# Backward attention loop: dS turned by the DMA alone, loads in groups, dK and dV stored once per head group

## The chip, the cores and the metric

The kernel runs on one core of a Trainium2 chip. The metric is device time in microseconds (us) of one execution, as a median of several runs. One more execution was taken by the hardware profiler; all durations, waits and busy shares come from that one, and its span is set beside the median of the runs below.

The engines of the core have their own instruction queues: TensorE (PE, with PEld for its weight loads), VectorE (DVE), ScalarE (ACT), GpSimd (POOL), and SyncE (SP), which only issues DMAs. A DMA that ScalarE issues stands in ScalarE's own queue between its other instructions.

## The reference

A transformer block (adaptive layer norm, multi-head attention, squared-ReLU MLP) is run forward, and all its gradients are computed. Sizes: 2048 tokens, model width 512, 32 heads of 16, hidden width 1792, bf16.

```python
def _A_ref(x, wqkv, wo):
    qkv = (x @ wqkv).reshape(B, S, 3, H, Dh).transpose(2, 0, 3, 1, 4)
    q, k, v = (qkv[0], qkv[1], qkv[2])
    scores = jnp.einsum('bhqd,bhkd->bhqk', q, k) * Dh ** (-0.5)
    p = softmax(scores, axis=-1)
    o = jnp.einsum('bhqk,bhkd->bhqd', p, v)
    return o.transpose(0, 2, 1, 3).reshape(B, S, D) @ wo
...
h = _layernorm(x) * (1 + ca) + sa
x = x + ga * _A_ref(h, A_wqkv, A_wo)
h = _layernorm(x) * (1 + cb) + sb
x = x + gb * _B_ref(h, B_w1, B_b1, B_w2, B_b2)
...
_out, _vjp = jax.vjp(_f, A_x, A_wqkv, A_wo, B_w1, B_b1, B_w2, B_b2, c, w_mod)
return (_out, *_vjp(grad_out))
```

The change concerns the gradient of the attention: with P the softmax and dP = dO V^T, dS = P * (dP - delta), and from it dQ = dS K, dK = dS^T Q and dV = P^T dO.

## The kernel before

The kernel has three parts in time: the forward pass with the MLP and its gradients (to about 1117 us), the backward attention loop (about 1117 to 2387 us), and a last stage that multiplies by the transposed wqkv, finishes the layer norm's gradient and forms the gradients of wqkv and w_mod (to the end).

**Tiling of the loop.** Heads are taken in eight groups of four (`hg`). For a group the keys are cut into four chunks of 512 (`kc`), the queries into four chunks of 512 (`qc`), and these into four tiles of 128 (`qi`). A *unit* is one (hg, kc, qc, qi): 128 queries by 512 keys by four heads. Four units with the same qc are a *block*; there are 512 units and 128 blocks, 16 blocks to a head group. Each operand of a group lies in a tile of 128 partitions, 32 to a head: 16 rows of data and one more that carries the softmax's normalization or delta, so that the matmul of scores already holds the shift and the matmul of dP already holds the subtraction of delta.

**One unit.** TensorE makes four score products (`score`, L1594, into one of three PSUM banks), ScalarE takes the exponential of each (`expo`, L1600, the tile `E_u`), TensorE makes dP for two heads at a time (`dp_pair`, L1614, `psD_u`), and VectorE multiplies the two (L1616, the tile `dS_u`, 128 x 1024 for two heads). `k_quad` (L1654) and `v_quad` (L1663) accumulate dK and dV of the group over all 16 query tiles in one bank, `accVK`, which ScalarE copies out for each key chunk into `vkb` (L1666).

**Turning dS.** dQ needs dS with keys on the partitions. Two units of a block share a `dS_u` tile (four such tiles go round), and after the second one SP issues a DMA transpose of the tile into `dsT` (L1631, 128 x 4096 bf16 or 1.05 MB; three `dsT` tiles go round, one for each block). So blocks with an even number make two such transposes. In blocks with an odd number (`on_pe`) the first two units go that way, the third goes by a DMA transpose of its own of half the size (L1629), and the fourth is turned on TensorE: `pe_turn` (L1644) makes eight 128 x 128 transposes into a PSUM bank, twice, and ScalarE copies each result out into `dsT` (L1760). A block's dQ (`dq_quad`, L1681, `dqacc`) is made two blocks later, ScalarE scales it into `dqtmp` or `dQacc` (L1694, L1691), and GpSimd adds it (L1699).

**Order.** The order of instructions on all five engines in the loop is written out by hand: two strings of tokens, `order_t` for the block after an odd one and `order_n` for the other. A token is a step: `s` a score, `e` an exponential, `D` a `dp_pair` with its product on VectorE and, after every other unit, the transpose; `q` a `k_quad` or `v_quad`; `d` half of a dQ; `Q` its eviction. Only `order_t` has `t` and `T` (TensorE's turn and its eviction) and `f` (`keep_warm`, filler matmuls, L1637). Both strings hold eight `D` for each block, so 128 to a head group.

**Transfers of the loop.** The calls `at(j, load, ...)` put a DMA behind the j-th `D`, in ScalarE's queue (`load`, L1576). `plan_head` plans the loads of the next head group: `kvq_loads` (q of the group with tokens on the partitions as `qs`, then k, q with its normalization row, v) and the rows of dO and delta; 22 loads, one every four `D`, from the 14th of the group before. Two sets of tiles (`hsets`) alternate between the groups. `spread_qz` (GpSimd) spreads `qs` into `qz` at `D` number 40 after that start. The finished dK and dV of a key chunk are stored four `D` after their eviction, 128 KB each time (`dVKtP`), and dQ of a group goes out in four stores from the sixth `D` after its last block (`dQc`). `head_loads` makes the loads of group 0 from SP's queue, before the loop, with the same `kvq_loads`. In the last group SP also loads finished gradients for the last stage.

All DMAs of SP and ScalarE draw their completion semaphores in turn from eight, so that a DMA first waits for the one that had its semaphore before it.

Of the kernel before, what the change touches and what calls it, by code (L numbers as in the profile page):

```python
# [34 lines left out]
def kernel(  # L35
# [9 lines left out]
    QC = n // 512  # L45
# [43 lines left out]
    q_st = dram.tile([HG, P, TT, 64], BF, name="q_st")  # L89
# [17 lines left out]
    dVKtP = dram.tile([HG, P, n], BF, name="dVKtP")  # L107
# [23 lines left out]
    def row_loads(dst, srcT, hg, cols, aux=None):  # L131
        for h in range(4):
            i = hg * 4 + h
            yield dst[32 * h:32 * h + DH, :], srcT[i * DH:(i + 1) * DH, cols]
        if aux is not None:
            yield dst.rearrange("(h c) n -> c h n", h=4)[DH], aux[hg * 4:(hg + 1) * 4, cols]
# [10 lines left out]
    with ExitStack() as ph:  # L147
# [969 lines left out]
        loads = {}  # L1117
# [85 lines left out]

        def kvq_loads(hg):
            hs = hsets[hg % 2]
            for i in range(4):
                yield hs["qs"][:, 4 * i:4 * i + 4, :], q_st[hg][:, 4 * i:4 * i + 4, :]
            yield from row_loads(hs["k"], qkT_st[1], hg, slice(0, n))
            yield from row_loads(hs["q"], qkT_st[0], hg, slice(0, n), m_st)
            yield from row_loads(hs["v"], vT_st, hg, slice(0, n))  # L1210
# [282 lines left out]
        with ExitStack() as ph2:  # L1493
            pools["mm"] = ph2.enter_context(tc.tile_pool(name="psM2", bufs=4, space=bass.MemoryType.PSUM))
            with tc.manual_schedule(engines={PE.engine, ACT.engine, DVE.engine, SP.engine, POOL.engine}):
# [28 lines left out]
                def head_loads():  # L1524
                    done = slice(0, 512 * (QC - 1))
                    for i, (to, fro) in enumerate(list(kvq_loads(0)) + list(row_loads(hsets[0]["do"][:, done], dOT_st, 0, done, d_st))):
                        later(i, sp, to, fro)
                    later(12, copy_const, qz[0].rearrange("p t h d -> p (t h d)"), 0.0)
                    later(16, spread_qz, 0)
# [18 lines left out]
    with ExitStack() as ph:  # L1548
# [7 lines left out]
        hst, bst, sst, dqt, cur = {}, {}, {}, {}, {}  # L1556
# [12 lines left out]
        def at(j, f, *args):  # L1569
            todo.setdefault(j, []).append((f, args))  # L1570
# [7 lines left out]
        def plan_head(hg):  # L1578
            j0 = (hg - 1) * 128 + 14
            loads = list(kvq_loads(hg)) + list(row_loads(hsets[hg % 2]["do"], dOT_st, hg, slice(0, n), d_st))  # L1580
            for i, (to, fro) in enumerate(loads):
                at(j0 + 4 * i, load, to, fro)
            at(j0 + 40, spread_qz, hg)

        banks = {"A": "ps0", "B": "ps1", "C": "px"}
# [16 lines left out]
        def dp_pair(u, pair):  # L1602
            hg, kc, qc, qi = units[u]
            st = hst[hg]
            qt = qc * 4 + qi
            if pair == 0:
                if qi % 2 == 0:
                    cur["dS"] = ework.tile([P, 2, 4, 512], BF, name="dS_u", tag="dS_u", bufs=4)
                bst[u][1] = cur["dS"][:, qi % 2]
            E_u, dS_u = bst[u]  # L1610
            psD = psd.tile([P, 2, 512], F32, name="psD_u", tag="pd")
            for hi in range(2):
                r = 32 * (2 * pair + hi)
                PE.matmul(psD[:, hi, :], st["do"][r:r + 32, qt * P:(qt + 1) * P], st["v"][r:r + 32, kc * 512:kc * 512 + 512],  # L1614
                          start=True, stop=True, tile_position=(r, 0))
            DVE.tensor_tensor(dS_u[:, 2 * pair:2 * pair + 2, :], psD[:], E_u[:, 2 * pair:2 * pair + 2, :], ALU.mult)  # L1616
            if qi == 3 and on_pe(u // 4):
                held["dS"] = dS_u

        def on_pe(b):  # L1620
            return b % 2 == 1

        def transpose_unit(u):
            hg, kc, qc, qi = units[u]
            if qi == 0:
                dqt[u // 4] = tpool.tile([P, 4, 16, P], BF, name="dsT", tag="dsT")
            if on_pe(u // 4) and qi >= 2:
                if qi == 2:
                    SP.dma_start(out=dqt[u // 4][:, qi], in_=bst[u][1].rearrange("p h k -> p (h k)"), transpose=True)  # L1629
            elif qi % 2 == 1:  # L1630
                SP.dma_start(out=dqt[u // 4][:, qi - 1:qi + 1].rearrange("p u b q -> p (u b) q"),  # L1631
                             in_=cur["dS"].rearrange("p u h k -> p (u h k)"), transpose=True)
# [24 lines left out]
        def v_quad(u):  # L1657
            hg, kc, qc, qi = units[u]
            qt = qc * 4 + qi
            E_u, dS_u = bst.pop(u)  # L1660
            acc = cur["vk"]
            for hq in range(4):
                PE.matmul(acc[32 * hq:32 * hq + DH, :], dOs_tok[:, qt, (hg * 4 + hq) * DH:(hg * 4 + hq + 1) * DH], E_u[:, hq, :],  # L1663
                          start=False, stop=(qt == TT - 1), tile_position=(0, 32 * hq), skip_group_check=True)
            if qt == TT - 1:
                ACT.activation(hst[hg]["vk"][:, kc * 512:(kc + 1) * 512], acc[:], AF.Identity)  # L1666
                if hg >= HG - 2:
                    xs["vk", hg] = hst[hg]["vk"]
                else:
                    part = slice(kc * 512, (kc + 1) * 512)  # L1670
                    at(cur["j"] + 4, load, dVKtP[hg][:, part], hst[hg]["vk"][:, part])

        def dq_quad(b, kt):
            hg, kc, qc, _ = units[4 * b]
# [40 lines left out]
        for hg in range(1, HG):  # L1715
            plan_head(hg)
# [3 lines left out]
        with tc.manual_schedule(engines={PE.engine, ACT.engine, DVE.engine, SP.engine, POOL.engine}):  # L1720
# [3 lines left out]
            idle = psx.tile([P, 512], F32, name="idle", tag="accVK")  # L1724
            for b in range(NU // 4 + 3):
                toks, bank = order_t if on_pe(b - 1) else order_n
                for tok in toks:
                    c, i = tok[0], int(tok[1:] or 0)
# [40 lines left out]
    with ExitStack() as ph:  # L1769
# [139 lines left out]
        with tc.manual_schedule(engines={PE.engine, ACT.engine, DVE.engine}):  # L1909
# [33 lines left out]
            for b in range(3):  # L1943
                for ic in range(DC):
                    dwqkv(b, ic)
                    i = b * DC + ic
# [75 lines left out]
```

## Time and profile before

| | us |
|---|---|
| median of 3 runs | 2488.03 |
| lowest, highest run | 2478.22, 2493.08 |
| the profiled execution's span | 2501.3 |
| PE busy in it | 2324.0 (93%) |
| ScalarE busy | 2303.7 (92%) |
| VectorE busy | 1837.7 (73%) |
| GpSimd busy | 488.0 (20%) |
| first to last dS product of the loop | 1116.9 to 2378.1 |
| granted TensorE clock, mean | 0.980 |

Busy shares are of the whole span: VectorE's 73% are a mean of about half in the forward pass and nearly all of the loop. DMA-issuing instructions count as busy on no engine; what holds SP's queue is seen only where that queue's own instructions are listed. In the rows of a tile or line, "SPq" and "ACTq" are instructions of the queues of SP and ScalarE, with their durations. Idle time of an engine is put down to what ended it.

### The profile page before, as it was taken

The page shows a single profiled execution, that of the slowest core. Times are in us where ns is not written, and L with a number is a line of the kernel's source. Part 1 is how long each engine was busy: PE and PEld are TensorE (multiplying, and loading weights), DVE is VectorE, ACT ScalarE, POOL GpSimd, SP SyncE. Part 2 cuts the span into 40 slices and gives each one's busy share as a digit, 9 for nine tenths or more (in the row PEclk, how much of TensorE's full clock was granted, in tenths as well). Part 3 has the DMA queues.
Part 4 walks back from the last instruction along what each step waited for, and adds up shares of the span by engine and source line. Part 5 has one row for each costly group of instructions (what it writes and reads, how often), then busy time and mean ns, then how long its engine had stood idle before and what let it go on. Part 6 is the DMA issues. An engine that isn't in the chain of part 4 may idle for free.

```text
span 2501.3 us, 49888 instructions
## 1 busy us (share of the span) xinstructions
PE 2324.0 (93%) x18948; PEld 783.4 (31%) x19036; DVE 1837.7 (73%) x2377; ACT 2303.7 (92%) x3560; POOL 488.0 (20%) x661
## 2 busy tenths in 40 slices
PE   8899899989998998999999999999999999999989
PEld 3232233223332333443223323233232323332344
DVE  6555354455435444579989999999999999999965
ACT  7999999999998999539999999999999999999944
POOL 2111223323533453110111101111011110110100
PEclk9999999999998999999999999999999999999999
DMA  4468463258546865979999999999999999999984
GB/s 146 130 167 176 144 150 97 88 166 142 98 95 142 151 131 110 256 200 196 201 192 206 199 198 202 196 204 203 205 205 198 205 202 199 200 198 214 201 253 133
DMA packets 1189503, 437.70 MB, mean 175 GB/s; under 512 B 1065867, under 2 KB 1160521, under 8 KB 1188878
## 3 DMA queue, kind: packets, MB, share of 16 engines
q1 hardware_dynamic: 1152414, 389.35, 79.0%
q0 software_dynamic: 19872, 27.09, 6.5%
q10 hardware_dynamic: 16976, 18.07, 2.9%
q8 instruction: 149, 2.44, 0.4%
q14 instruction: 92, 0.75, 0.1%
HBM read 98.30 MB, written 70.80 MB: 68 GB/s over the span
## 4 chain that ended last, share of the span: by engine, by line
ACT 40%; PE 38%; issue 8%; DVE 7%; DMA 3%; SPq 1%; ACTq 1%; POOL 0%; DVEq 0%; another core or an unknown queue 0%; POOLq 0%
ACT E_u L1600 24%; ACT ET L578 12%; PE dqacc L1681 4%; PE psST L576 3%; PE psS_A L1594 3%; PE accVK L1654 2%; PE pm L233 2%; ACT dsT L1760 2%; PE psS_B L1594 2%; PE pdh L1858 2%; PE oacc L592 2%; PE psS_C L1594 2%; PE pwq L1892 2%; PE pm L500 2%; PE pm L410 2%
## 5 line engine op out<-in xcount | busy, mean ns | idle before, releaser
L1616 DVE TENSOR_TENSOR dS_u<-psD_u,E_u 128x1024 bf16<-128x1024 f32 x1024 | 1185.9, 1218 | 77.1 <-PE psD_u L1614 30.2
L578 ACT ACTIVATE ET<-psST 128x1024 bf16<-128x1024 f32 x1024 | 941.9, 1242 | 16.6 <-PE psST L576 16.3
L1600 ACT ACTIVATE E_u<-psS_A 128x512 bf16<-128x512 f32 x768 | 509.9, 664 | 10.8 <-PE psS_C L1594 8.5
L1600 ACT ACTIVATE E_u<-psS_B 128x512 bf16<-128x512 f32 x768 | 503.2, 655 | 10.8 <-DMA dsT<-dS_u 2.7
L1614 PE MATMUL psD_u<-iv,ido 32*128 32x512 bf16 x2048 | 409.1, 388 | 1.5 <-DVE dS_u L1616 1.3
L576 PE MATMUL psST<-qt_sb,kt_sb 32*128 32x512 bf16 x2048 | 313.8, 386 | 48.0 <-ACT ET L578 41.0
L1600 ACT ACTIVATE E_u<-psS_C 128x512 bf16<-128x512 f32 x512 | 334.3, 653 | 3.1 <-PE psS_B L1594 1.1
L1594 PE MATMUL psS_B<-ik,iq 32*128 32x512 bf16 x768 | 296.1, 386 | 11.7 <-ACT E_u L1600 4.4
L1594 PE MATMUL psS_A<-ik,iq 32*128 32x512 bf16 x768 | 294.5, 383 | 11.0 <-DVE dwlast L237 1.0
L1699 POOL TENSOR_TENSOR dQacc<-dQacc,dqtmp 128x512 f32<-128x512 f32 x64 | 81.2, 1268 | 858.8 <-ACT dqtmp L1694 797.4
L1594 PEld LDWEIGHTS <-iq 32*128 32x128 bf16 x2048 | 129.7, 91 | 313.9 <-issue 296.9
L1654 PE MATMUL accVK<-dS_u,qz 128*32 128x512 bf16 x2048 | 213.5, 388 | 0.5 <-PE psD_u L1614 0.2
L592 PE MATMUL oacc<-ET,vaug 128*32 128x512 bf16 x2048 | 207.0, 394 | 3.9 <-DVE ostage L596 3.9
L1663 PE MATMUL accVK<-E_u,dOs_tok 128*16 128x512 bf16 x2048 | 204.5, 388 | 0.0
L1594 PE MATMUL psS_C<-ik,iq 32*128 32x512 bf16 x512 | 194.2, 379 | 4.5
L576 PEld LDWEIGHTS <-kt_sb 32*128 32x128 bf16 x2048 | 84.3, 91 | 328.2 <-issue 306.5
L1681 PE MATMUL dqacc<-dsT,KS_tok 128*32 128x512 bf16 x2048 | 145.7, 382 | 18.8 <-DMA dsT<-dS_u 5.0
L1760 ACT ACTIVATE dsT<-ptT 128x1024 bf16<-128x1024 bf16 x128 | 144.1, 1126 | 13.1 <-PE ptT L1644 12.2
L251 DVE COPY part<-pm 128x512 f32<-128x512 f32 (+2 forms) x106 | 65.2, 615 | 121.9 <-PE pm L233 111.8
L1614 PEld LDWEIGHTS <-ido 32*128 32x128 bf16 x2048 | 105.2, 91 | 101.3 <-issue 94.9
L1654 PEld LDWEIGHTS <-qz 128*32 128x32 bf16 x2048 | 58.5, 94 | 178.0 <-issue 162.9
L1699 POOL TENSOR_TENSOR dQst<-dQacc,dqtmp 128x512 bf16<-128x512 f32 x32 | 40.6, 1270 | 266.1 <-ACT dqtmp L1694 266.1
(415 smaller groups left out, 2688.7 us busy)
## 6 DMA issues: line engine op xcount, KB each, us to landing
p_st<-part POOLq DMA_DIRECT2D x36, 256.0 KB, 4.6
kt_sb<-qkT_st POOLq DMA_DIRECT2D x124, 64.0 KB, 3.0
wA<-in_B_w_dram SPq DMA_DIRECT2D x28, 256.0 KB
wB<-w1T_st SPq DMA_DIRECT2D x21, 256.0 KB
wA<-w2T_st SPq DMA_DIRECT2D x21, 256.0 KB
wB<-in_B_w_dram SPq DMA_DIRECT2D x21, 256.0 KB
p_st<-part POOLq DMA_DIRECT2D x28, 192.0 KB, 4.6
p_st<-part SPq DMA_DIRECT2D x18, 256.0 KB
```

The lines of the kernel that those rows point to most:

```text
L576: PE.matmul(ps[:, hi, :], kt_sb[r:r + 32, kt * P:(kt + 1) * P], qt_sb[r:r + 32, :], start=True, stop=True, tile_position=(r, 0))
L578: ACT.activation(ET[:, 2 * pair:2 * pair + 2, :], ps[:], AF.Exp, scale=SCALE)
L592: PE.matmul(oacc[32 * hq:32 * hq + 32, :], lhsT, ET[:, hq, :], start=(kt == 0), stop=(kt == TT - 1), tile_position=(0, 32 * hq), skip_grou ...
L1594: PE.matmul(psS[:], st["q"][r:r + 32, qt * P:(qt + 1) * P], st["k"][r:r + 32, kc * 512:kc * 512 + 512], start=True, stop=True, tile_positi ...
L1600: ACT.activation(bst[u][0][:, hq, :], sst.pop((u, hq))[:], AF.Exp, scale=SCALE)
L1614: PE.matmul(psD[:, hi, :], st["do"][r:r + 32, qt * P:(qt + 1) * P], st["v"][r:r + 32, kc * 512:kc * 512 + 512], start=True, stop=True, til ...
L1616: DVE.tensor_tensor(dS_u[:, 2 * pair:2 * pair + 2, :], psD[:], E_u[:, 2 * pair:2 * pair + 2, :], ALU.mult)
L1654: PE.matmul(cur["vk"][32 * hq:32 * hq + 32, :], hst[hg]["qz"][:, qt, hq, :], bst[u][1][:, hq, :], start=(qt == 0), stop=False, tile_positi ...
L1663: PE.matmul(acc[32 * hq:32 * hq + DH, :], dOs_tok[:, qt, (hg * 4 + hq) * DH:(hg * 4 + hq + 1) * DH], E_u[:, hq, :], start=False, stop=(qt ...
L1681: PE.matmul(acc[32 * hq:32 * hq + 32, :], KS_tok[:, kc * 4 + kt, h * DH:h * DH + 32], tT[:, :, hq * 4 + kt, :], start=(kt == 0), stop=(kt ...
L1699: POOL.tensor_tensor(dst2, dst, tmp[:], ALU.add)
L1760: ACT.activation(dst, pt[:], AF.Identity)
```

## The change

Four edits. All blocks use `order_n`, since `on_pe` now returns False: a block makes two DMA transposes of full size, TensorE turns nothing, and the filler matmuls of `order_t` are gone. `qs` of a group is loaded by one DMA instead of four. The loads of the next group, now 19, are issued in four groups of 5, 5, 4 and 5, one load for each `D` within a group, the groups beginning 26 `D` apart. dK and dV of a group are stored by one DMA of 512 KB, five `D` after the last eviction, instead of four.

```diff
         def kvq_loads(hg):
             hs = hsets[hg % 2]
-            for i in range(4):
-                yield hs["qs"][:, 4 * i:4 * i + 4, :], q_st[hg][:, 4 * i:4 * i + 4, :]
+            yield hs["qs"][:], q_st[hg]
             yield from row_loads(hs["k"], qkT_st[1], hg, slice(0, n))
             yield from row_loads(hs["q"], qkT_st[0], hg, slice(0, n), m_st)
             yield from row_loads(hs["v"], vT_st, hg, slice(0, n))
...
         def plan_head(hg):
             j0 = (hg - 1) * 128 + 14
             loads = list(kvq_loads(hg)) + list(row_loads(hsets[hg % 2]["do"], dOT_st, hg, slice(0, n), d_st))
-            for i, (to, fro) in enumerate(loads):
-                at(j0 + 4 * i, load, to, fro)
+            for g, part in enumerate((slice(0, 5), slice(5, 10), slice(10, 14), slice(14, 19))):
+                for i, (to, fro) in enumerate(loads[part]):
+                    at(j0 + 26 * g + i, load, to, fro)
             at(j0 + 40, spread_qz, hg)
...
         def on_pe(b):
-            return b % 2 == 1
+            return False
...
                 if hg >= HG - 2:
                     xs["vk", hg] = hst[hg]["vk"]
-                else:
-                    part = slice(kc * 512, (kc + 1) * 512)
-                    at(cur["j"] + 4, load, dVKtP[hg][:, part], hst[hg]["vk"][:, part])
+                elif kc == QC - 1:
+                    at(cur["j"] + 5, load, dVKtP[hg], hst[hg]["vk"][:])
```

## The prediction

> **What bounds the kernel now.** I read the page first, then busy time by stage, then the rows of the tile dsT (the transposed dS), and last the SP queue and VectorE in order of time.
>
> The page gives the span and the costliest groups:
>
> ```profile
> span 2501.3 us, 49888 instructions
> ...
> L1616 DVE TENSOR_TENSOR dS_u<-psD_u,E_u 128x1024 bf16<-128x1024 f32 x1024 | 1185.9, 1218 | 77.1 <-PE psD_u L1614 30.2
> ...
> L1760 ACT ACTIVATE dsT<-ptT 128x1024 bf16<-128x1024 bf16 x128 | 144.1, 1126 | 13.1 <-PE ptT L1644 12.2
> ```
>
> A group's row has its count, then busy us and mean ns of one, then the engine's idle time before it. L1760 is the eviction of the dS tiles that TensorE turns (L1644, 1024 transposes, 83.9 us of PE in the by-line view). The backward loop runs from 1117 us, when VectorE forms its first dS, to about 2387 us. Busy time by stage in it (columns: window, its length, then busy us and instructions of each engine, TensorE's granted clock, DMA share, GB/s):
>
> ```profile
> 1437.00:1750.00 313.00, 301.68 (x2884) 94.08 (x2880) 296.22 (x257) 307.19 (x586) 35.91 (x26) 0.98 1.19 201
> 1750.00:2065.00 315.00, 301.67 (x2884) 93.88 (x2881) 296.69 (x257) 307.02 (x586) 35.91 (x26) 0.98 1.18 203
> ```
>
> PE, VectorE and ScalarE are each busy for 94 to 98% of the stage, and the DMA share is over 1: on this reading everything is full, and taking work from PE and ScalarE ought to pay. But the queue that feeds the transposes is in none of these columns. The tile view of dsT has it (min/median/max of one, in ns):
>
> ```profile
> L1631 SPq DMA_TRANSPOSE dsT<-dS_u x192: 4766/5266/6831, 1123.7 to 2377.1; - x192
> L1629 SPq DMA_TRANSPOSE dsT<-dS_u x64: 1759/2336/4402, 1140.0 to 2382.1; - x64
> ```
>
> A full transpose (L1631, two query tiles of four heads, 1.05 MB) holds SP for 5.27 us in the median, a half one (L1629) for 2.34 us. The next transpose does not begin before the one ahead has let go of SP. SP in order of time:
>
> ```profile
> 1677.73 3.05 SPq L1629 DMA_TRANSPOSE dsT<-dS_u  x1
> 1680.87 16.46 SPq L1631 DMA_TRANSPOSE dsT<-dS_u  x3
> 1697.43 1.77 SPq L1629 DMA_TRANSPOSE dsT<-dS_u  x1
> 1699.36 17.32 SPq L1631 DMA_TRANSPOSE dsT<-dS_u  x3
> 1716.78 3.07 SPq L1629 DMA_TRANSPOSE dsT<-dS_u  x1
> 1719.93 15.94 SPq L1631 DMA_TRANSPOSE dsT<-dS_u  x3
> 1735.96 1.83 SPq L1629 DMA_TRANSPOSE dsT<-dS_u  x1
> ```
>
> Three full and one half in each pair of blocks, and SP has hardly 0.1 us between them: 1677.73 + 3.05 = 1680.78, and the next begins at 1680.87. VectorE in order of time has the other pace:
>
> ```profile
> 1621.18 18.75 DVE L1616 TENSOR_TENSOR dS_u<-psD_u,E_u 128x1024 bf16<-128x1024 f32 x16 [0.37 <-ACT dQacc L1691]
> ```
>
> Sixteen products, a pair of blocks, in 18.75 us. The 64 pairs take 1260.3 us on SP (first transpose begins at 1123.72, last ends at 2384.00), 19.69 us each. So the loop is balanced: VectorE needs 18.75 us of each 19.69, and SP, summing the single records (192 full ones 1021.9 us, mean 5.32; 64 half ones 162.0 us, mean 2.53), needs 3 x 5.32 + 2.53 + 4 x 0.1 = 18.9. Set against the end of the dS that each one reads, transposes begin 1.5 us late in the median and up to 10 us late; the half one is what lets SP catch up.
>
> **The change, part by part.**
>
> *dS no longer turned on TensorE.* `on_pe` is false, so every block runs `order_n` and the sixteenths that L1644/L1760 turned go to SP. Off: 1024 transposes (83.9 us of PE), 128 evictions (144.1 us of ScalarE), and the filler matmuls of `order_t`. On: 64 half transposes become full ones. Per pair of blocks SP then needs 4 x 5.32 + 4 x 0.1 = 21.7 us, against VectorE's 18.75. The 228 us taken from PE and ScalarE are worth nothing on the path, because SP's queue is late next: TensorE's dqacc (L1681) waits for dsT, behind it in TensorE's order stand the next scores and dP products, and ScalarE's exponentials and VectorE's dS wait for those; the four dS_u buffers close the ring. When dqacc of a block waits, the next block's two transposes already stand on SP, so SP itself does not run dry. Term: 64 x 21.7 - 1260.3 = 1388 - 1260 = **+128 us**.
>
> Its bounds go by what one transpose costs when SP has no pause. Queued ones (under 0.3 us behind the one ahead) average, pause included, 5.44 us for 1.05 MB over 213 cases; in the last four and first blocks of each head, without loads, 5.28; in the others 5.51. The first of all, on an idle queue, took 4.83 us, the fastest 4.77. From 5.28 x 256 = 1352 us (+91) to 5.51 x 256 = 1411 us (+150); I take 5.42, the mean of all with the pause, as the loop has both kinds of block.
>
> [...]
>
> *Loads in dense groups, q_st whole, dK/dV stored once.* Per head group ScalarE's queue issues 19 loads instead of 22 and one 512 KB store instead of four of 128 KB; bytes are the same. At 0.31 to 0.34 us an issue (ScalarE's queue in order of time) 21 + 18 fewer issues are 13 us off ScalarE, covered by SP's bound, so nothing; if that cover were gone, at most -13. What they cost the transposes is 5.51 - 5.28 = 0.23 us on each of about 22 per head, 40 us in all. Thirty transfers per head become 24: I take a fifth off, **-8 us, rounded to -5** since the bytes stay. Bounds: -40 (all of it goes) to +40 (bunching doubles it; single transposes beside the dQ stores and the dK/dV store took 6.69 and 6.83 us). The deadlines hold: the last load leaves at D 82 after j0 instead of 84, and the next head needs it at 114.
>
> *A wait that gets denser.* At each head boundary five loads and four dQ stores now leave within some eleven D steps. DMAs go round eight completion semaphores, so in the instruction order the second dQ store waits for a transpose issued just ahead of the loads. Such waits are there already:
>
> ```profile
> L1576 ACTq DMA_DIRECT2D dQc<-dQst x28: 308/378/2076, 1299.7 to 2246.9; - x28
> ```
>
> the longest issue took 2.08 us for a median of 0.38. With SP some 10 us late it can hold ScalarE, and the exponentials behind it, that long. SP keeps about one queued transpose meanwhile, so I take 0; bounds 0 to 7 x 5 = +35 us.
>
> *Head group 0's loads* on SP before the loop lose three issues and move up by three ticks: -1 to +2 us, I take 0. *The end:* SP's loads for the last stage (first at 2384.06) stay right behind the last transpose and move with it: 0.
>
> Sum: 2501.3 + 128 - 5 = 2624 us for a profiled execution. The profile stands 13.3 us over the median of 2488.0 shown, so the runs should give 2624 - 13 = **2611 us**, 4.9% slower.
>
> **The rivals.**
>
> *Bubbles on top of it.* The ScalarE wait above lasts until a transpose has landed while SP has nothing left, and SP pays for a refill of one to two dS pairs, 5 to 10 us in each of seven heads: 2646 to 2681 us. For: in-order ScalarE, longest wait 2.08 us already. Against: one transpose is queued behind the one waited for.
>
> *SP fits after all, other side.* What I count as SP's cost is partly back-pressure from plain transfers, and with fewer, wider ones a transpose falls to its floor, 4.77 + 0.1 = 4.87 us. Then 256 x 4.87 = 1247 us, 13 less than now: 2475 us. It decides below 4.92 us each (1260.3 / 256). For: 4.8 to 4.9 us occur often. Against: the blocks with no loads still average 5.28.
>
> *Transposes are not the limit.* The queue runs only as fast as dS arrives, so SP has room to go faster once dS comes faster. Then VectorE sets the pace, 64 x 18.75 = 1200 us: 60 less, 2428 us. Against: transposes are late behind dS with SP never pausing, as in the SP rows above. [...]
>
> *It doesn't turn everything on the DMA.* The instruction order has 256 full transposes and no `ptT`; no chance.
>
> **How the numbers follow.** SP-bound as summed 0.80 (own range 2570 to 2650), bubbles 0.12, SP fits 0.05, transposes no limit 0.03. The range leaves out the two small cases below and the far end of the bubbles: 2560 to 2660. About 0.5% (12 us) is what a measurement of this kernel can tell from no change; it lies between 2475.6 and 2500.5. SP fits is split between its floor (2475, faster by just over 0.5%) and a little above it: 0.02 and 0.03. So faster 0.05, same 0.03, slower 0.92.
>
> **What would show it.** Right: SP's DMA_TRANSPOSE x256 with a median of 5.2 to 5.6 us and no pause; first to last about 1383 us; VectorE's idle time before L1616 up from 77 to some 200 us; the chain of waits with far more of "DMA dsT<-dS_u" than its 3% of DMA; ScalarE's busy share in the loop down from 97% to about 80%. Wrong: pauses on SP, a median under 4.9 us, or transposes beginning right as dS ends. Bubbles: dQ store issues of 5 us and more on ScalarE's queue with SP idle behind them.

## The result, and the profile after

The changed kernel takes 2665.4 us in the median (2654.6 to 2669.8), the kernel before 2490.6 us in the runs beside it: a ratio of 1.070, with a 95% interval of 1.068 to 1.073. The forecast was slower, at 2611 us with a range of 2560 to 2660. The direction and the main mechanism hold, but the time lies 5 us above the range and 54 us above the forecast.

The page after, span and the costliest groups that answer to those of before (count, then busy us and mean of one, then idle time before it and what ended most of it):

```profile
span 2667.0 us, 47155 instructions
...
L1616 DVE TENSOR_TENSOR dS_u<-psD_u,E_u 128x1024 bf16<-128x1024 f32 x1024 | 1197.0, 1219 | 230.8 <-PE psD_u L1614 196.6
...
L1680 PE MATMUL dqacc<-dsT,KS_tok 128*32 128x512 bf16 x2048 | 204.5, 485 | 109.3 <-DMA dsT<-dS_u 59.2
```

The products on VectorE are as long as before (1219 ns), but the idle time ahead of them went from 77 to 231 us. dQ's matmuls now stand idle for 109 us, 59 of them for the DMA transpose of dS. Before it was 18.8 us:

```profile
L1681 PE MATMUL dqacc<-dsT,KS_tok 128*32 128x512 bf16 x2048 | 145.7, 382 | 18.8 <-DMA dsT<-dS_u 5.0
```

No eviction of TensorE's transposes is left.

Busy time by stage of the loop, same columns as before:

```profile
1437.00:1750.00 313.00, 255.63 (x2252) 63.53 (x2252) 262.09 (x226) 250.74 (x488) 30.79 (x22) 0.84 1.17 200
1750.00:2065.00 315.00, 257.48 (x2223) 62.24 (x2216) 258.57 (x222) 246.75 (x478) 30.58 (x23) 0.82 1.17 199
```

PE, VectorE and ScalarE fell from 94 to 98% to 78 to 84% of the stage. DMA share and GB/s stand where they stood. TensorE's granted clock fell from 0.98 to 0.83, which the forecast had not foreseen.

The transposes in the tile view (min/median/max in ns), and SP's queue in order of time:

```profile
L1631 SPq DMA_TRANSPOSE dsT<-dS_u x256: 4705/4992/8796, 1122.3 to 2549.0; - x128
```

```profile
1697.84 106.73 SPq L1631 DMA_TRANSPOSE dsT<-dS_u  x20
```

Twenty transposes in 106.73 us, one after the other, 5.34 us each: SP has no pause of note in this stretch, as forecast. From first to last it takes 2555.7 - 1122.3 = 1433.4 us, where 1383 was forecast. The single records add up to 256 x 5.342 = 1367.6 us, and the pauses between them to 65.8 us. The mean was forecast at 5.32, the pauses at 256 x 0.1 = 25.6 us. Of the pauses, 43.5 us are in 35 that last over 0.3 us: four behind the first four transposes of the loop (11 us), and 29 us ahead of the first ten transposes of the later seven heads.

### The profile page after: what moved, and what is told of

Its sections match the earlier page's. It is cut to its first block, busy times and chain, and to the rows that moved or that the text cites. A ratio compares the mean times of both kernels' runs of the same rounds, so it can differ in the third digit from the quotient of the medians.

```text
span 2667.0 us, 47155 instructions
## 1 busy us (share of the span) xinstructions
PE 2317.4 (87%) x17755; PEld 693.5 (26%) x17755; DVE 1848.9 (69%) x2377; ACT 2217.7 (83%) x3432; POOL 488.1 (18%) x661
## 4 chain that ended last, share of the span: by engine, by line
PE 45%; ACT 27%; DMA 14%; issue 7%; DVE 6%; POOL 0%; ACTq 0%; DVEq 0%; POOLq 0%; SPq 0%
ACT E_u L1600 14%; DMA dsT<-dS_u 12%; ACT ET L578 11%; PE dqacc L1680 6%; PE psS_B L1594 4%; PE psS_A L1594 4%; PE psS_C L1594 3%; PE accVK L1654 3%; PE psST L576 3%; PE accVK L1663 3%; PE pm L233 2%; PE oacc L592 2%; PE pm L500 2%; PE pdh L1857 2%; PE pwq L1891 2%
## 5 line engine op out<-in xcount | busy, mean ns | idle before, releaser
L1616 DVE TENSOR_TENSOR dS_u<-psD_u,E_u 128x1024 bf16<-128x1024 f32 x1024 | 1197.0, 1219 | 230.8 <-PE psD_u L1614 196.6
L1600 ACT ACTIVATE E_u<-psS_B 128x512 bf16<-128x512 f32 x768 | 472.0, 615 | 125.3 <-PE psD_u L1614 98.3
L1600 ACT ACTIVATE E_u<-psS_C 128x512 bf16<-128x512 f32 x640 | 395.9, 619 | 104.8 <-PE psS_B L1594 62.0
L1614 PE MATMUL psD_u<-iv,ido 32*128 32x512 bf16 x2048 | 457.4, 443 | 0.8 <-DVE dS_u L1616 0.8
L1600 ACT ACTIVATE E_u<-psS_A 128x512 bf16<-128x512 f32 x640 | 397.5, 621 | 32.3 <-PE psD_u L1614 17.9
L1594 PE MATMUL psS_B<-ik,iq 32*128 32x512 bf16 x768 | 339.5, 442 | 28.8 <-ACT E_u L1600 17.5
L1594 PE MATMUL psS_C<-ik,iq 32*128 32x512 bf16 x640 | 270.4, 422 | 96.9 <-ACT E_u L1600 95.3
L1680 PE MATMUL dqacc<-dsT,KS_tok 128*32 128x512 bf16 x2048 | 204.5, 485 | 109.3 <-DMA dsT<-dS_u 59.2
L1654 PE MATMUL accVK<-dS_u,qz 128*32 128x512 bf16 x2048 | 238.1, 452 | 1.1 <-DVE dS_u L1616 0.9
L1663 PE MATMUL accVK<-E_u,dOs_tok 128*16 128x512 bf16 x2048 | 226.8, 433 | 0.0
L1680 PEld LDWEIGHTS <-KS_tok 128*32 128x32 bf16 x2048 | 40.9, 100 | 229.3 <-issue 192.9
```

The source lines that it names most:

```text
L1594: PE.matmul(psS[:], st["q"][r:r + 32, qt * P:(qt + 1) * P], st["k"][r:r + 32, kc * 512:kc * 512 + 512], start=True, stop=True, tile_positi ...
L1600: ACT.activation(bst[u][0][:, hq, :], sst.pop((u, hq))[:], AF.Exp, scale=SCALE)
L1654: PE.matmul(cur["vk"][32 * hq:32 * hq + 32, :], hst[hg]["qz"][:, qt, hq, :], bst[u][1][:, hq, :], start=(qt == 0), stop=False, tile_positi ...
L1680: PE.matmul(acc[32 * hq:32 * hq + 32, :], KS_tok[:, kc * 4 + kt, h * DH:h * DH + 32], tT[:, :, hq * 4 + kt, :], start=(kt == 0), stop=(kt ...
```

## The experiments

"Per head" below is the time from a head group's first dS product to the next one's; a pair is two blocks, an eighth of it.

**The turn alone, and the moves alone.** The change has two halves, and each was run by itself.

```diff
 # the kernel before, with
         def on_pe(b):
-            return b % 2 == 1
+            return False
```

> The kernel before with on_pe false alone; loads and stores as before. Theory S (SP's issue of 256 full transposes at 5.3 to 5.4 us sets the loop, and pauses on SP add to it): most of the change's cost is here, first to last transpose 1400 to 1435 us, time 2635 to 2665 us, ratio 1.058 to 1.070. Rival L (the denser loads and the one large store hold the transposes up): the turn alone costs what was forecast for it, about 1383 us on SP, 2600 to 2620 us. Under both the granted clock of the loop tells whether the turn alone makes TensorE cold: about 0.8 if so, over 0.95 if the grouped loads do it.

Measured: 2630.3 us (2623.6 to 2639.2), ratio 1.056 (1.054 to 1.059), so 140 us of the 175. Per head 173.2 us on average, 21.65 us a pair: the 21.7 of the forecast. First to last transpose 1396 us. The transposes and a stage of the loop:

```profile
L1631 SPq DMA_TRANSPOSE dsT<-dS_u x256: 4678/5192/8211, 1118.5 to 2507.2; - x128
```

```profile
1437.00:1750.00 313.00, 266.68 (x2293) 64.49 (x2289) 268.07 (x231) 256.03 (x496) 31.14 (x23) 0.84 1.20 207
```

SP's queue is late all the way: set against the end of the dS that each one reads, 244 of the 256 transposes begin more than 0.3 us late, 3.8 us in the median. By time the run lies between S and L. The clock in the loop is 0.84 (0.906 over the whole span, against 0.972 with the moves alone, below), so it is the turn, not the loads, that makes TensorE's clock fall. The turn also takes out the filler matmuls of `order_t` (L1637: 266 before, 11 after), so whether the waits or the missing fillers do it is not told apart here.

```diff
 # the changed kernel, with
         def on_pe(b):
-            return False
+            return b % 2 == 1
```

> The changed kernel with on_pe as before (odd blocks turn a quarter on TensorE): only the loads, q_st whole and the one dK/dV store are changed. Theory S: SP has 1.0 us of slack in each pair of blocks, so 2478 to 2500 us, within 0.5% of before. Rival L: the bunched loads stall ScalarE at each of seven head boundaries by 4 to 8 us and make single transposes 6 to 9 us long, 2515 to 2545 us.

Measured: 2540.6 us, ratio 1.021 (1.019 to 1.023): L, 50 us slower than before. The clock stays at 0.95 to 0.96 in the middle of the loop. The second pair of a head takes 28.2 us on average (heads 1 to 6), all others 19.2 to 19.9. That is the place where five loads and four dQ stores now leave one after the other. ScalarE in order of time there (start, duration, what, idle time before it):

```profile
1791.46 0.31 ACTq L1575 DMA_DIRECT2D ik<-qkT_st  x1
1791.87 1.10 ACTq L1575 DMA_DIRECT2D dQc<-dQst  x1
1793.01 0.60 ACT L1600 ACTIVATE E_u<-psS_B 128x512 bf16<-128x512 f32 x1 [0.91 <-PE ptT L1644]
...
1794.89 0.62 ACT L1600 ACTIVATE E_u<-psS_B 128x512 bf16<-128x512 f32 x1
1800.83 0.31 ACTq L1575 DMA_DIRECT2D dQc<-dQst  x1
1801.24 0.60 ACT L1600 ACTIVATE E_u<-psS_A 128x512 bf16<-128x512 f32 x1 [5.74 <-DMA dsT<-dS_u]
```

The second dQ store leaves only at 1800.83, and the exponential behind it has stood 5.74 us, released by a DMA transpose. ScalarE has no use for that transpose's data. In the single records the store waits for the completion semaphore with number 105. SP's transpose from 1787.69 to 1794.92 had drawn it last, so the store waits until that transpose has landed. SP in the same stretch:

```profile
1776.18 18.73 SPq L1631 DMA_TRANSPOSE dsT<-dS_u  x3
1794.97 4.94 SPq L1629 DMA_TRANSPOSE dsT<-dS_u  x1
1800.07 14.90 SPq L1631 DMA_TRANSPOSE dsT<-dS_u  x2
```

The three full ones took 6.2 us each instead of 5.3, the last of them 7.2, so the store waited for a transpose that was itself late. Over the loop such waits add up, in the waits of that kernel (us in total, times, longest), to

```profile
ACT E_u L1600 <- DMA dsT<-dS_u: 30.2, 8, 5.7
```

The first profile of the kernel before has one such wait, of 2.7 us, and the second none. On SP's queue the 50 us divide about evenly. From first to last transpose it takes 1300.5 us, 49 more than in the second profile of the kernel before (1251.6, below): 25 of them are longer transposes and 24 are pauses between them.

**Which of the moves.** Five kernels take them apart, all with on_pe as before.

```diff
 # the moves alone, with
-                    at(cur["j"] + 6 + hq, load, dQc[hg // 2, r:r + DH, :], ...)
+                    at(cur["j"] + 18 + hq, load, dQc[hg // 2, r:r + DH, :], ...)
```

> The kernel with the moved loads and on_pe as before (2541 us), and the four dQ stores of a head 12 D steps later. Theory W (a cluster of nine DMAs in ScalarE's queue comes round to a completion semaphore that a just issued transpose still holds, so ScalarE stands 3 to 6 us and the second pair of blocks of each head takes 27 to 29 us instead of 19 to 20): the second pair falls back to 20 to 21 us and the time to 2488 to 2505 us. Rival T (the dense transfers themselves hold the transposes up): the cluster's cost stays, 2525 to 2540 us.

Measured: 2520.3 us, ratio 1.012 (1.011 to 1.014): 20 of the 50 us come back, between the two theories. ScalarE's waits for a transpose fall to

```profile
ACT E_u L1600 <- DMA dsT<-dS_u: 7.6, 3, 4.8
```

but the second and third pairs still take 21.8 and 22.6 us, and a full transpose 5.46 us on average, against 5.30 in a second profile of the kernel before: 192 x 0.16 = 31 us, as much as the 30 us that are left, though SP's pauses are also 11 us shorter than there.

```diff
 # the kernel before, with
-            for i in range(4):
-                yield hs["qs"][:, 4 * i:4 * i + 4, :], q_st[hg][:, 4 * i:4 * i + 4, :]
+            yield hs["qs"][:], q_st[hg]
...
-                else:
-                    part = slice(kc * 512, (kc + 1) * 512)
-                    at(cur["j"] + 4, load, dVKtP[hg][:, part], hst[hg]["vk"][:, part])
+                elif kc == QC - 1:
+                    at(cur["j"] + 5, load, dVKtP[hg], hst[hg]["vk"][:])
```

> The kernel before with q_st loaded whole and dK/dV stored once, but the loads spaced four D steps apart as before and on_pe as before. Theory W: no cluster but the old one of dQ stores and loads, 2480 to 2500 us. Rival V (the one store of 512 KB, 128 rows of 4 KB, is what stalls the transposes at the boundary): 2510 to 2540 us.

Measured: 2502.8 us, ratio 1.0052 (1.0038 to 1.0065): 12 us, between the two theories. Against it, the moves alone (2540.6) differ in one thing, the dense groups: the same 19 loads from the same first `D`, the same one store. So the grouping by itself costs 38 us, and the 12 go with loading q_st whole or with the one store. The second half of that edit alone:

```diff
 # the kernel before, with
-                else:
-                    part = slice(kc * 512, (kc + 1) * 512)
-                    at(cur["j"] + 4, load, dVKtP[hg][:, part], hst[hg]["vk"][:, part])
+                elif kc == QC - 1:
+                    at(cur["j"] + 5, load, dVKtP[hg], hst[hg]["vk"][:])
```

> The kernel before with dK/dV of a head stored once (512 KB), all else as before. The kernel with this and q_st loaded whole took 12.5 us more than before. Theory V (the one store stands in front of the boundary's transposes): 2498 to 2505 us. Rival Q (the whole load of q_st does it): 2485 to 2493 us.

Measured: 2488.6 us, ratio 1.001 (0.9999 to 1.0022): the one store costs nothing that can be seen, V is out and the time is the one of Q.

```diff
 # the kernel before, with q_st loaded whole, and
-            for i, (to, fro) in enumerate(loads):
-                at(j0 + 4 * i, load, to, fro)
+            for g, part in enumerate((slice(0, 5), slice(5, 10), slice(10, 14), slice(14, 19))):
+                for i, (to, fro) in enumerate(loads[part]):
+                    at(j0 + 26 * g + i, load, to, fro)
```

> The kernel before with q_st loaded whole and the loads in four dense groups, dK/dV stored in four parts as before, on_pe as before. If the edits add up (2541 us with both, 50 us over before, 12 of them without the groups): 2522 to 2532 us. If the groups cost only together with the one store, all within the same eleven D steps of a head boundary: 2490 to 2505 us.

Measured: 2541.0 us, ratio 1.022 (1.020 to 1.023): neither case, since both gave less. The groups cost what all moves together cost, and need no help from the store.

```diff
 # the kernel before, with q_st loaded whole, and
-            for i, (to, fro) in enumerate(loads):
-                at(j0 + 4 * i, load, to, fro)
+            for g, part in enumerate((slice(0, 5), slice(5, 10), slice(10, 14), slice(14, 19))):
+                for i, (to, fro) in enumerate(loads[part]):
+                    at(j0 + 12 + 22 * g + 4 * i, load, to, fro)
```

> The kernel before with q_st loaded whole and the loads four D steps apart as before, but the first one twelve D steps later, behind the dQ stores. Theory W/T (what costs is transfers close together at the boundary, whether through ScalarE's wait or through SP's transposes): 2478 to 2488 us, a little better than before. If the old arrangement loses nothing at the boundary: 2486 to 2495 us.

Measured: 2492.3 us, ratio 1.0017 (1.0007 to 1.0027). The same 19 loads, four D apart and behind the dQ stores: the 50 us are gone, but nothing is gained over before. This run changes both the spacing and the place; that the density costs, not the number, rests on the 38 us above, where the spacing alone differs.

**What one transpose costs by itself.** A kernel of its own, cut to its loops:

```python
for i in range(32):
    turn(i)                      # SP: DMA transpose of 128 x 4096 bf16
for i in range(32):
    turn_half(i)                 # 128 x 2048
...
for i in range(32):
    turn(i)
    for k in range(2):
        ACT.activation(pace[:], pace[:], AF.Identity)
    ACT.dma_start(out=rows[...], in_=row_st[...])    # 16 rows of 4 KB; then the same with stores
```

> A kernel of its own with nothing of the reference's computation (its outputs are zeros): 32 full transposes and 32 half ones on SP with nothing beside them, then 32 full ones beside paced 64 KB row loads from ScalarE's queue, then 32 beside paced 64 KB row stores. Theory S: a full one costs 4.8 to 4.9 us with nothing beside it, since SP can issue no faster, and a half one 2.4 to 2.5. Rival B (in the loop, other traffic makes up most of the 5.3 us): 3.6 to 4.0 us alone. For the moved loads: each load or store adds 0.2 to 0.8 us to the transpose beside it if the transfers themselves hold transposes up, under 0.1 us if only the waits of ScalarE do.

The loads and stores did not stand where they were meant to: in ScalarE's queue all 64 left ahead of the pacing activations and ran beside the first 32 transposes, the loads from 17.5 to 86.6 us and the stores from 86.6 to 170 us, closer together than meant. So the last 64 transposes had no transfer beside them. SP's queue, first beside the stores, then alone:

```profile
88.56 72.14 SPq L60 DMA_TRANSPOSE full<-src  x12
```

```profile
297.37 104.20 SPq L60 DMA_TRANSPOSE full<-src  x21
```

Alone, that is with no other transfer beside it, a full one takes 104.20 / 21 = 4.96 us, pause included, and a half one 2.50. B had 3.6 to 4.0, so B is out; S had 4.8 to 4.9 and is right within 0.1 us. Beside the stores it is 72.14 / 12 = 6.0 us; over all of them, pause included, it is 5.50 us on average beside the loads and 5.98 beside the stores. Thirteen transposes with 32 loads beside them make (5.50 - 4.96) x 13 / 32 = 0.22 us for each 64 KB load; fourteen with 32 stores 0.45 us for each 64 KB store. 256 x 4.96 = 1270 us is 10 to 18 us more than the loop took in the two profiles of before: even at this price, without any loads and stores beside them, the transposes from this one queue would not have made the loop faster.

Is it SP's issuing or the DMA engines behind it that sets the 4.96 us? The trace holds every packet that the DMA engines moved, 256 bytes each for a transpose and 4096 to a full one. With nothing beside them 847 of these finish in the median microsecond. Beside the loads, 20 of 70 single microseconds finish more than 1000, and one finishes 1136. In the loop of the changed kernel the median is 840, one microsecond in six has more than 1000, and the most is again 1136. So the engines did finish more in some microseconds than in the median one with nothing beside them: that speaks for SP's issuing as what sets the 4.96 us, but does not show it.

**The share turned on TensorE as a dial.**

```diff
 # the kernel before, with
-            return b % 2 == 1
+            return b % 4 == 1
```

> The kernel before with on_pe for every fourth block instead of every second; loads and stores as before. Theory S (two limits: TensorE, ScalarE and VectorE at 19.3 us a pair of blocks, SP at 4 x 5.4 = 21.7 us a pair with no half transpose, 18.9 with one in each pair; the larger sets the loop): one half transpose in two pairs, 20.3 us a pair on average, 64 x 20.3 = 1300 us, 2535 to 2550 us, about 0.35 of the way from before to the turn alone. Rival B (each sixteenth moved to the DMA costs the same, bandwidth): half way, 2560 us.

Measured: 2564.1 us, ratio 1.030 (1.027 to 1.034): 76 of 140 us, the half way of B, not S. On SP's queue past the first head, a pair of blocks with a half transpose takes 19.0 us on average, 0.5 of it pauses, and a pair without one 22.3, 1.3 of it pauses. S had 18.9 and 21.7. (The profiled execution took 2571.1 us, 7 over the median.) So S misses by pauses of SP in the dear pairs, and by the first head, which takes 176.2 us where the next six take 164.8 on average. Why SP pauses there is not shown. The time alone would speak for B, bandwidth; the packets above speak against the DMA engines as the limit.

**Is it the cold TensorE?** With six filler matmuls to a block:

```diff
 # the changed kernel, order_n with an f behind six of the eight q
-            "s0 D s1 q e0 q s2 e1 e2 D s3 s4 q s5 e3 D e4 "
+            "s0 D s1 q f e0 q f s2 e1 e2 D s3 s4 q f s5 e3 D e4 "
...
-            "s11 e10 D q s12 e11 e12 s13 e13 D q s14 s15 e14 e15 D q ").split()
+            "s11 e10 D q f s12 e11 e12 s13 e13 D q f s14 s15 e14 e15 D q f ").split()
```

> The changed kernel with six filler matmuls (zeros onto accVK, as order_t had) in each block of order_n. Theory C (half clock makes TensorE slower than SP, 12.6 us a block against 10.7, and so SP runs dry): granted clock in the loop from 0.82 to over 0.93, pauses on SP from 43.5 to under 15 us, 2630 to 2640 us. Rival W: clock up or not, the pauses at the boundaries stay and the time with them, 2655 to 2670 us. If the fillers cost TensorE more than the clock gives, over 2670 us.

Measured: 2660.7 us (2656.6 to 2662.4), ratio 1.068 (1.067 to 1.070). A stage of its loop:

```profile
1437.00:1750.00 313.00, 259.24 (x2436) 66.36 (x2435) 264.30 (x227) 252.35 (x488) 30.82 (x22) 0.92 1.19 202
```

The clock rose from 0.84 to 0.92 and the time stayed within 5 us, where W had it: C falls as a cause of the lost time. Pauses of over 0.3 us fell from 43.5 to 28.9 us, and a full transpose went from 5.34 to 5.37 us. A clock of 0.84 costs little here, since SP is the one waited for.

```diff
 # the changed kernel, with
-                    at(cur["j"] + 6 + hq, load, dQc[hg // 2, r:r + DH, :], ...)
+                    at(cur["j"] + 18 + hq, load, dQc[hg // 2, r:r + DH, :], ...)
```

> The changed kernel, with the four dQ stores of a head 12 D steps later, so that they no longer stand among the first five loads of the next head. Theory W (the dQ store's wait for a transpose's completion semaphore stops ScalarE at the head boundary, SP runs dry and TensorE goes cold after it): the pauses in positions 3 to 9 after a boundary vanish, about 32 us of the 43.5 us of pauses, 2630 to 2640 us. Rival C (TensorE's clock falls anyway, since it waits for dsT in every block): pauses stay, at most the 13 us of the first pause of each boundary go, 2650 to 2665 us.

Measured: 2657.2 us, ratio 1.068 (1.066 to 1.069). Pauses over 0.3 us fell from 43.5 to 17.6 us as W had it, and the second pair from 30.5 to 23.0 us, but a full transpose went from 5.34 to 5.39 us and the other pairs rose. Of 24 us of pauses that are gone from SP's queue, longer transposes took 12 back, and the time is 8 us shorter: the one that C gave, though the pauses went as W said.

**GpSimd's queue instead of ScalarE's.**

```diff
         def load(to, fro):
-            ACT.dma_start(out=to, in_=fro)
+            POOL.dma_start(out=to, in_=fro)
```

On the changed kernel:

> The changed kernel with the loop's loads and stores issued from GpSimd's queue instead of ScalarE's. Theory W: ScalarE no longer stands behind a transpose's semaphore at any of the four groups, the second pair of blocks of a head falls from 30 to 22 us, and what is left is SP's issue: per head 172 to 175 us as with the turn alone, 2620 to 2635 us. Rival T (the dense transfers hold the transposes up whoever issues them): 2650 to 2670 us.

Measured: 2644.6 us, ratio 1.064 (1.061 to 1.067), some 21 us better, between the two theories. The four executions spread from 2642.2 to 2663.4 us, and the profiled one is the slowest of them, so its trace does not show where the 21 us come from. In it the second pair of a head still takes 27.6 us, not 22: there the dense transfers cost though ScalarE does not issue them. On the kernel before:

> The kernel before with the loop's loads and stores issued from GpSimd's queue instead of ScalarE's. Theory W: the old kernel has such waits too, but short ones (dQ store issues of up to 2.1 us), and pairs of 20.5 us beside the usual 19.3: 2470 to 2485 us. If ScalarE's waits play no part before: 2485 to 2495 us. If GpSimd's own issuing is dearer for the DMA engines: over 2495 us.

Measured: 2507.3 us, ratio 1.0079 (1.0066 to 1.0092): 17 us slower, the third case. Full transposes take 5.47 us on average, against 5.30 in the second profile of the kernel before, so in this loop transfers issued from GpSimd hold them up more. Why is not shown.

**Two questions about the kernel before.**

> The kernel before once more, for a second profile of it. If the 13.3 us by which its first profile stood over the median lay in the loop (pairs of 20.5 us among those of 19.3), a run of 2485 to 2495 us has first to last transpose in 1245 to 1252 us instead of 1260. If it lay elsewhere, the loop is 1260 us again and the rest shorter.

Measured, without any edit: 2492.3 us, span 2490.5, first to last transpose 1251.6 us. Of the 10.8 us between the two spans (2501.3 and 2490.5), 8.7 lay in the loop.

```diff
 # the kernel before, with
-                    at(cur["j"] + 6 + hq, load, dQc[hg // 2, r:r + DH, :], ...)
+                    at(cur["j"] + 6 + 8 * hq, load, dQc[hg // 2, r:r + DH, :], ...)
```

> The kernel before with the four dQ stores of a head eight D steps apart instead of one, so that no cluster of DMAs is left in ScalarE's queue. Theory W: the second pairs of heads (20.6 us on average against 19.3) come down, six or seven times 1 to 2 us: 2476 to 2486 us. If the old cluster costs nothing: 2486 to 2493 us.

Measured: 2496.0 us, ratio 1.0029 (1.0010 to 1.0049): slower than either case. The old cluster costs nothing, and spreading it is slightly worse. No version tried beats the kernel before.

## Why the prediction was right, and where it was wrong

**SP's queue as the bound: right.** The forecast read 21.7 us a pair off the mean of the single transposes; the turn alone runs at 21.65. That it fits so well is in part luck: in the turn alone a transpose takes 5.28 us and not 5.32, and the pauses add up to 44.6 us and not 25.6, and the two nearly cancel. That PE's and ScalarE's 228 us would be worth nothing held as well: ScalarE has 20% of the stage idle and the loop is longer. Of the signs named, VectorE's idle time (231 us for some 200), ScalarE's share (78 to 80% for about 80%) and DMA's share in the chain of waits (14%, 12 of them the transposes of dS, 3% before) came true. The median, 4.99 us where 5.2 to 5.6 was named, did not, nor did SP run without a pause. With no other transfer beside it (`m1_transposes`), the transpose moves 1.05 MB in 4.96 us, 211 GB/s; in the loop before it took 5.27 us in the median.

**Profile against median: wrong by about 10 us.** The forecast subtracted the 13.3 us by which its profile stood over the median. Most of that excess was in the loop, and the loop is what SP's time replaces: an absolute 1388 us takes the excess with it. Set against the second profile, the turn is 1388 - 1252 = 136 us, and 2488 + 136 = 2624, where 2630 was measured. The start has about as much as the rest: the first pair takes 30 us instead of 24.

**The loads: the step that failed.** "Thirty transfers per head become 24: I take a fifth off, -8 us, rounded to -5" counted transfers. Measured: +35 us on top of the turn (2665 - 2630), +50 without it, with the bounds at 40. This term is 40 of the 54 us by which the forecast was off; 12 are the turn's (140 for 128) and 2.5 the median of the kernel before. What counts is how close together the loads leave: without the turn the spacing alone makes 38 us, with the number and the bytes unchanged. On SP's queue, from the turn alone to all four edits, the time from first to last transpose grows by 37.6 us (1395.8 to 1433.4): 16 are longer transposes (5.28 to 5.34 us), 21 are pauses. The kernel for the transposes by themselves shows a price for each transfer beside one (0.22 and 0.45 us). That spread loads fit into what a pair of blocks has to spare, and five and four in a row do not, is argued from these numbers, not shown by itself.

**"I take 0" for the denser wait: wrong as well, inside its bounds.** ScalarE stood 30.2 us for transposes in the moves alone, and moving the dQ stores away gave 20 us back there, and 8 us with the turn. The reason given, that SP keeps a queued transpose meanwhile, overlooked that at a boundary transposes are themselves slow: in the changed kernel two or three of the first four of each later head take 5.8 to 8.8 us. The rival of bubbles (2646 to 2681 us, given 0.12) has the measured time in its range, and its mechanism is in the trace, but smaller: ahead of the first ten transposes of the later heads SP pauses 29 us, and 6 in the turn alone. That is 3 us more in each of seven heads, where the rival had 5 to 10. So it accounts for a part of the 35 us. Its sign, dQ store issues of 5 us and more, did not show: the longest took 1.09 us, and the wait stands as idle time ahead of the store.

**Sum by what was measured:** 2490.6 + 140 (turn, a run of its own) + 35 (the rest) = 2665.6. The 35 is what is left over, not a second measurement; the moves by themselves cost 50, so the two halves share some 15 us.

Left open: why loading q_st whole seems to cost some 11 us (2502.8 with the one store, 2488.6 with the store alone) when it stands near the dQ stores and 4 us when it comes later; by the profiles it lies in the second pair of a head (22.3 us against 20.2). Open too is how much of the pauses and of the longer transposes on SP's queue comes from ScalarE's waits, since the two move against each other when one is taken away.

## What to carry to other kernels

Look at the queue that issues transfers as at an engine: add up its instructions' own durations in the stage, since busy shares don't show it; here three engines at 94 to 98% beside it did not tell what bound next. Price a change in when transfers leave by what stands beside them, not by their number: this loop, where SP needs 18.9 us of each 19.6, took up spread transfers (2492.3 and 2502.8 us) and not bunched ones (2540.6 and 2541.0). When a new bound gives the stage an absolute time, set that against the rest of the profile, and do not carry the old stage's deviation along.

## What was not expected of the hardware

With no other transfer beside it, a full transpose takes 4.96 us and a half one 2.50, and plain 64 KB transfers beside it add 0.22 (load) and 0.45 us (store) each. The DMA engines finished 847 of the transposes' packets in the median microsecond alone and up to 1136 in one beside the loads; that SP's issuing sets the pace is the reading of this, not shown by itself. TensorE's granted clock fell from 0.98 to 0.83 in a loop where TensorE is still busy for 82% of the time, and raising it to 0.92 changed the time by less than 5 us in 2665.
